# Attention products with one input in PSUM, GpSimd products in short pieces, replanned dummies and one opening load queue

## The chip, the cores and the metric

One NeuronCore of a Trainium2 chip runs the whole kernel. Its engines are TensorE (PE; its weight loads are PEld), VectorE (DVE), ScalarE (ACT), GpSimd (POOL) and SyncE (SP). The metric is device time in microseconds (us) of one execution. A profile is taken from one more execution; its span leaves out a little time at either end.

## What is computed

Two blocks in a row: linear attention with a quadratic sketch as its feature map, and then a feed-forward layer with the activation h - tanh(h). Batch 4, 4 heads, sequence 1088, head size 32, sketch size 8; 4352 tokens of width 128, hidden width 2048; all float32 at the ends.

```python
def phi(x):                                   # S1, S2: 8 x 32
    a = np.einsum('rd,bhsd->bhsr', S1, x)
    b = np.einsum('rd,bhsd->bhsr', S2, x)
    return np.einsum('bhsi,bhsj->bhsij', a, b).reshape(*x.shape[:-1], 64)
q_p, k_p = phi(q), phi(k)
kv, z = np.einsum('bhsf,bhsd->bhfd', k_p, v), np.sum(k_p, axis=2)
num = np.einsum('bhsf,bhfd->bhsd', q_p, kv)
den = np.einsum('bhsf,bhf->bhs', q_p, z)[..., None] + 1e-06
x = num / den                                 # laid out as 4352 x 128
h = x @ w_in                                  # 128 x 2048
out = (h - np.tanh(h)) @ w_out                # 2048 x 128
```

## The kernel before

**A planner writes the order.** Every operation is entered with P.op: engine, estimated cost in ns, the data it reads and writes (from which its dependencies follow), and a priority (`prio`, lower is sooner, in slots of the feed-forward layer). `listed` lays the operations out on the five engines by these costs, starting at each step the ready operation with the lowest priority; VectorE may stay idle for a short while (HOLD) if a more urgent operation is about to be ready. `schedule` repeats this six times and keeps the shortest plan. `P.line` adds an order by hand between tagged operations. `sync` puts in the semaphore waits; each engine then runs its list strictly in order. So what the plan puts ahead of an instruction is ahead of it on the chip, however long it takes there. A load is modelled as 2000 ns after its issue plus its size on one shared bus.

**Work by group.** The 34 chunks of 32 tokens of each batch are split into three groups (SIZES: 8, 14, 12 in batch 0, and so on), twelve in all, g = 0 to 11. A group of n = 256 to 448 columns has: p{g} (16 small PE matmuls, `quarters`, L589) that project q into PSUM banks 0 and 1; VectorE's transposition qq (L618), product au (L621), sum dn (L624); a PE matmul ds (L631) into bank 2; VectorE's reciprocal rd (L634) and scaling an (L636, both inputs in SBUF); the outer products qp (L641), one half on GpSimd and one on VectorE, in one instruction each; their transpositions qpT (L648); w{g} (16 matmuls, L602) into banks 2 and 3; and the cast xT (L655, tags x{g}). w{g} and p{g+1} are one operation of the plan, so the cast of x{g} waits for both.

**Keys by batch** (`keys`, `sums_of`). kT (L484) transposes the keys, 8 + 8 or 16 PE matmuls project them (L491) into banks 0 and 1, kab (L502) transposes that into SBUF. From kab come the 64 products per token and head, wk (L509): both inputs are views of kab in SBUF. In batch 0 VectorE makes parts 0 to 1, 2 to 3 and 4 of nine, GpSimd 5 to 8 in one instruction; later VectorE makes three parts and GpSimd six, in one instruction each. Beside it gram (L520), mask product gm (L527, one input in PSUM), fold (L534) and u (L539) fill in a part of wq that p needs. sums (L551, 72 matmuls, needs all of wk and v), kvz, turn and ndw (L557 to L563) give the matrix that w needs.

**Feed-forward** (`layers`). Per group sixteen matmuls L710 (w_in) into one of three PSUM banks, sixteen tanh on ScalarE (L713), and sixteen matmuls L721 (w_out) that accumulate in bank 7 with a lag of 12 slots; the linear part h @ w_out is a precomputed product (wt, wc, wp at L675 to L686; whi and wlo) added with two matmuls L702. Then osb (L728) and four stores.

**Opening.** The S matrices are loaded on SP, k of batch 0 on ScalarE's queue, q of the first group and w_in on SP, v split over both. 90 dummy matmuls on zeros (L445, priority 5000, planned at 107 ns) fill PE where the plan has nothing else. The sketch matrix pS (L449) and wkm (L452) stand ahead of all key work; for VectorE a line gives wkm, kT00, kT01, qT0, s2m, kab0, wk00, gm0, wk02, u0, wk04, qq0 and on; for PE pS to w1p2.

## Time and profile before

| | us |
|---|---|
| median of three runs | 125.65 (124.51 to 125.68) |
| the profiled execution | 126.7 |
| its span | 124.2 |
| TensorE, VectorE, ScalarE, GpSimd busy in it | 110.0, 77.1, 80.5, 32.6 |
| start of the first xT cast | 20.95 |

All times in rows are us from the start of the span unless marked ns. "idle before <-releaser" is how long the engine did nothing ahead of a row, and what ended that; "issue" there means that the profile shows nothing it waited for. A row that groups instructions gives the first start and the time over which they lie. PE ends are modelled, so a busy PE is not PE at its peak. PEclk is the granted TensorE clock as a share of its full 2.4 GHz; 0.50 is the other level, 1.2 GHz.

### The profile page before, as it was taken

The numbers are of one execution on the slowest core, as the hardware profiler recorded it, in microseconds if no ns is written. First come the engines' busy times: TensorE is split into PE (matmuls) and PEld (weight loads), VectorE is DVE, ScalarE is ACT, GpSimd is POOL, SyncE is SP. The second block draws the span as 40 slices with busy tenths as digits, with TensorE's granted clock in tenths as the row PEclk, the third lists the DMA queues.
The fourth block names the chain that finished last, engine by engine and source line by source line (L and its number), as shares of the span: only waits on it lengthen the run. The fifth ranks groups of instructions, "written<-read, shape, count | busy, mean of one in ns | idle before, by whom it ended". The sixth has DMA issues, their size and how long they took to land.

```text
span 124.2 us, 3347 instructions
## 1 busy us (share of the span) xinstructions
PE 110.0 (89%) x1392; PEld 62.8 (51%) x1392; DVE 77.1 (62%) x170; ACT 80.5 (65%) x207; POOL 32.6 (26%) x40
## 2 busy tenths in 40 slices
...
DMA packets 24623, 11.23 MB, mean 90 GB/s; under 512 B 18720, under 2 KB 22944, under 8 KB 24608
## 3 DMA queue, kind: packets, MB, share of 16 engines
...
q10 hardware_dynamic: 576, 0.82, 2.2%
...
q14 instruction: 4, 0.03, 0.1%
...
## 4 chain that ended last, share of the span: by engine, by line
PE 66%; DVE 19%; ACT 6%; issue 3%; POOL 2%; DVEq 0%
PE ps L710 18%; PE ps L721 18%; PE ps L445 8%; DVE wk L509 6%; ACT tt L713 6%; PE ps L602 5%; DVE an L636 4%; PE ps L551 4%; PE ps L589 3%; PE ps L702 3%; PE ps L491 3%; DVE kab L502 3%; POOL qp L641 2%; DVE qpT L648 1%; DVE osb L728 1%
## 5 line engine op out<-in xcount | busy, mean ns | idle before, releaser
L713 ACT ACTIVATE tt<-ps 128x384 bf16<-128x384 f32 (+3 forms) x192 | 73.6, 500 | 19.0 <-PE ps L710 18.7
L710 PE MATMUL ps<-xT,w_in 128*128 128x384 bf16 (+3 forms) x192 | 58.8, 322 | 1.1 <-ACT tt L713 0.3
L721 PE MATMUL ps<-tt,w_out 128*128 128x384 bf16 (+3 forms) x192 | 53.2, 322 | 0.0
L710 PEld LDWEIGHTS ps<-xT,w_in 128*128 128x128 bf16 x192 | 18.3, 98 | 24.6 <-ACT tt L713 15.4
L641 POOL TENSOR_TENSOR qp<-an,qq 128x384 f32<-128x384 f32 (+3 forms) x12 | 13.9, 1159 | 57.9 <-DVE an L636 57.9
L721 PEld LDWEIGHTS ps<-tt,w_out 128*128 128x128 bf16 x192 | 19.4, 102 | 8.7 <-issue 2.5
L509 POOL TENSOR_TENSOR wk<-kab 128x1536 f32<-128x1536 f32 (+1 forms) x4 | 12.4, 3110 | 13.6 <-DVE kab L502 13.6
L445 PE MATMUL ps<-wz 128*128 128x256 bf16 x90 | 13.7, 301 | 2.1 <-DVE hmask L422 1.1
L648 DVE STREAM_TRANSPOSE qpT<-qp 128x384 f32<-128x384 f32 (+3 forms) x24 | 13.0, 545 | 1.0 <-POOL qp L641 0.2
L655 DVE CAST xT<-ps 128x384 bf16<-128x384 f32 (+3 forms) x12 | 6.4, 536 | 11.6 <-PE ps L589 11.6
L445 PEld LDWEIGHTS ps<-wz 128*128 128x128 bf16 x90 | 9.1, 108 | 5.5 <-issue 2.5
L728 DVE STREAM_TRANSPOSE osb<-ps 128x384 f32<-128x384 f32 (+3 forms) x12 | 6.4, 535 | 7.2 <-PE ps L710 4.5
L634 DVE RECIPROCAL rd<-ps 128x24 f32<-128x24 f32 (+3 forms) x12 | 3.6, 297 | 11.2 <-PE ps L631 11.1
L509 DVE TENSOR_TENSOR wk<-kab 128x768 f32<-128x768 f32 (+2 forms) x6 | 8.6, 1436 | 0.1
L636 DVE TENSOR_TENSOR an<-qq,rd 128x96 f32<-128x96 f32 (+3 forms) x12 | 7.4, 619 | 0.4
L589 PE MATMUL ps<-qT,wq 64*32 64x192 f32 (+3 forms) x192 | 6.6, 331 | 1.1 <-DVE wq L539 1.1
L618 DVE STREAM_TRANSPOSE qq<-ps 128x384 f32<-128x384 f32 (+3 forms) x12 | 6.6, 549 | 0.3 <-PE ps L589 0.3
L602 PE MATMUL ps<-qpT,ndw 64*32 64x192 f32 (+3 forms) x192 | 6.6, 328 | 0.2
L641 DVE TENSOR_TENSOR qp<-an,qq 128x384 f32<-128x384 f32 (+3 forms) x12 | 6.4, 535 | 0.4
L557 ACT COPY kvz<-ps 128x128 f32<-128x128 f32 x4 | 1.1, 266 | 8.2 <-PE ps L551 8.2
L573 DVE STREAM_TRANSPOSE qT<-qraw 128x384 f32<-128x384 f32 (+3 forms) x12 | 6.2, 518 | 0.0
L702 PE MATMUL ps<-xT,whi 128*128 128x384 bf16 (+3 forms) x12 | 3.9, 321 | 2.5 <-DVE osb L728 2.5
...
## 6 DMA issues: line engine op xcount, KB each, us to landing
...
w_in_f<-in_moe_w_in_dram SPq DMA_DIRECT2D x4, 256.0 KB, 5.4
...
```

The lines of the kernel that those rows point to most:

```text
L445: P.op("tensor", cost, lambda e: e.matmul(ps[:, 6, 0:256], wz[:, 0:128], wz[:, :], start=True, stop=True), r=[("wz",)], w=[bank[6]], prio= ...
L509: P.op(eng, (dve if eng == "vector" else pool)(64 * n), lambda e: e.tensor_tensor(out=wk[:, t0:t1, :, :].rearrange("p t h (i j) -> p (t h) ...
L589: ins = e.matmul(ps[32 * s:32 * s + 32, r, 0:32 * nh], wq[64 * r:64 * r + 64, b, y, :, :].rearrange("p h x -> p (h x)"), qT[i][64 * r:64 * ...
L602: ins = e.matmul(ps[32 * h:32 * h + 32, 2 + u, 0:32 * nh], ndw[i][64 * u:64 * u + 64, 32 * h:32 * h + 32], src[64 * u:64 * u + 64, h // 2, ...
L636: P.op("vector", dve(4 * n), lambda e: e.tensor_tensor(out=an[u][:, 0:n, :], in0=a[:, 0:n, 0:4], in1=rd[u][:, 0:n, None].to_broadcast([128 ...
L641: P.op("gpsimd" if r else "vector", (pool if r else dve)(32 * m), lambda e, lo=lo, m=m: e.tensor_tensor(out=qp[u][:, lo:lo + m, :].rearran ...
L648: P.op("vector", dve(32 * m), lambda e, lo=lo, m=m: e.transpose(out=qpT[u][:, 32 * lo:32 * (lo + m)], in_=qp[u][:, lo:lo + m, :].rearrange ...
L702: P.op("tensor", pe(n), lambda e, x=x, f=front and x is whi, l=not front and x is wlo: e.matmul(acc[:, 0:n], x[:, :], xT[:, t0:t0 + n], st ...
L710: P.op("tensor", pe(n), lambda e, jb=jb, bk=bk: e.matmul(bk[:, 0:n], w_in[:, 128 * jb:128 * jb + 128], xT[:, t0:t0 + n], start=True, stop= ...
L713: P.op("scalar", act(n), lambda e, ts=ts, bk=bk: e.activation(out=tt[:, ts, 0:n], in_=bk[:, 0:n], func=AF.Tanh, scale=-1.0), r=[kb], w=[(" ...
L721: P.op("tensor", pe(n), lambda e, jb=jb, ts=ts: e.matmul(acc[:, 0:n], w_out[:, jb, :], tt[:, ts, 0:n], start=(jb == 0 and not g), stop=(jb ...
L728: P.op("vector", dve(n), lambda e: e.transpose(out=osb[u][:, 0:n], in_=acc[:, 0:n]), r=[ka], w=[("osb", u)], prio=slot0)
```

## The change

- **Products with an input in PSUM.** In batch 0 VectorE transposes the first 256 columns of the projection a second time, into PSUM bank 2 (kps), and its two remaining wk products take their second input there. rd is now written to PSUM, so `an` reads one input there. For groups 0 and 1 `an` is cut in two, and the half that VectorE multiplies on itself lies in PSUM too.
- **GpSimd.** In batch 0 it makes wk part 4, parts 5 to 6 and parts 7 to 8, in three instructions; in later batches all nine parts in nine. From group 2 on it makes both halves of qp.
- **Banks and order.** ds moves to bank 0; the keys of later batches use banks 2 and 3; qq has two buffers in place of three. w{g} and p{g+1} are two operations, in this order. wt0 stands ahead of sums0 and wt1 ahead of turn0 on PE, wc0 ahead of kvz0 and wc1 ahead of ndw0 on ScalarE.
- **Dummies.** 80 in place of 90, planned at 213 ns for the first 17 and 125 after. One is not started if an urgent operation will be ready within its cost, and all that the plan has after w0 are dropped (`trim`).
- **Loads.** Loads of one queue keep the order in which they are entered. q of the first group and all of v for batch 0 move to ScalarE's queue behind k; the first w_in load waits until k has landed. The planner's load model is 1400 ns after issue, with rates by kind of load.

```diff
+    def trim(self):
+        order = self.schedule()["tensor"]
+        n = order.index(self.tags["w0"])
+        late = {o for o in order[n:] if o.prio >= FILL}
...
-            if o.sem is None and e in HELD:
+            if o.sem is None and (e in HELD or o.prio >= FILL):
                 hold = None
+                most = 1.0 if o.prio >= FILL else HOLD
...
-        o = P.op(eng, size / 330, fn, w=() if also else keys, sem=sem, prio=prio)
+        chain = queue.setdefault(eng, [])
+        o = P.op(eng, size / rate, fn, r=r, w=() if also else keys, sem=sem, prio=prio)
...
+        if chain:
+            o.order.add(chain[-1])
...
-        return ((0, 2), (2, 4), (4, 5), (5, 9)) if b == 0 else ((0, 3), (3, 9))
+        return ((0, 2), (2, 4), (4, 5), (5, 7), (7, 9)) if b == 0 else tuple((t, t + 1) for t in range(9))
...
-            (-24, -990), (-15, -985), (-14, -980), (-12, -960), (-12, -975), (-11, -970))]
-        kb = bank[0:2]
-        gb = 4 if b == 0 else 1
+            (-24, -990), (-15, -985), (-14, -980), (-2, -960), (-12, -975), (-11, -970))]
+        k0 = 2 if b else 0
+        kb = bank[k0:k0 + 2]
+        gb = 4 if b == 0 else 3
...
+        if b == 0:
+            P.op("vector", dve(256), lambda e: e.transpose(
+                out=ps[:, 2, 0:256].rearrange("p (t r x) -> p r t x", t=4, r=2),
+                in_=ps[:, 0:2, 0:128].rearrange("p r (t j) -> p r t j", j=32)),
+                r=kb, w=[bank[2]], prio=T[2], tag="kps")
...
-            ab = kab[:, t0:t1, :, :, :, :].rearrange("p t r h i x -> p (t r h) i x")
+            ab = bv = kab[:, t0:t1, :, :, :, :].rearrange("p t r h i x -> p (t r h) i x")
+            if eng == "vector":
+                bv = ps[:, 2, 64 * t0:64 * t1].rearrange("p (n i x) -> p n i x", i=R, x=2)
...
-            mul("gpsimd" if t1 == 9 else "vector", t0, t1, T[3])
+            mul("vector" if b == 0 and t1 <= 4 else "gpsimd", t0, t1, T[3])
...
+        half = g < 2
+        p_rd, p_an = ps[:, 0, 288:288 + n], ps[:, 1, 256:256 + 4 * m].rearrange("p (n x) -> p n x", x=4)
...
+                out=out, in0=a[:, lo:hi, 0:4], in1=p_rd[:, lo:hi, None].to_broadcast([128, hi - lo, 4]), op=ALU.mult),
...
-            P.op("gpsimd" if r else "vector", (pool if r else dve)(32 * m), lambda e, lo=lo, m=m: e.tensor_tensor(
+            dv = half and not r
+            P.op("vector" if dv else "gpsimd", (dve if dv else pool)(32 * m), lambda e, lo=lo, dv=dv: e.tensor_tensor(
...
-    warm(90, 107, 5000)
+    warm(80, 5000)
     load_k(0, -2995, "scalar")
-    load_q(0, -2990, (0,))
-    load_v(0, -2980, ("sync", "scalar", "sync", "scalar"))
+    load_q(0, -2990, (0,), "scalar")
+    load_v(0, -2980, ("scalar",) * 4)
     for x in range(4):
-        load_w_in(x, -960)
+        load_w_in(x, -960, [("kraw", 0, 1)] if x == 0 else ())
...
-        quarters([("w", g)] + ([("p", g + 1)] if g + 1 < NG else []), T)
+        quarters([("w", g)], T)
         x_of(g, T)
+        if g + 1 < NG:
+            quarters([("p", g + 1)], T + 0.1)
+            P.line([f"w{g}", f"p{g + 1}"])
...
-    P.line(["cin0", "cin1", "cin2", "cin3", "kvz0", "ndw0", "wc0", "wc1"])
-    P.line(["wk05", "qp01", "cout0", "cout1"])
+    P.line(["cin0", "cin1", "cin2", "cin3", "wc0", "kvz0", "wc1", "ndw0"])
+    P.line(["wk04", "wk05", "wk07", "qp01", "cout0", "cout1"])
```

## Rows read from the trace of the kernel before

**Rows 1.** The page, busy us, share of the span and instructions of each engine
```profile
PE 110.0 (89%) x1392; PEld 62.8 (51%) x1392; DVE 77.1 (62%) x170; ACT 80.5 (65%) x207; POOL 32.6 (26%) x40
```

**Rows 2.** Chain of waits that ended last, shares by line, from the page
```profile
PE ps L710 18%; PE ps L721 18%; PE ps L445 8%; DVE wk L509 6%; ACT tt L713 6%; PE ps L602 5%; DVE an L636 4%; PE ps L551 4%; PE ps L589 3%; PE ps L702 3%; PE ps L491 3%; DVE kab L502 3%; POOL qp L641 2%; DVE qpT L648 1%; DVE osb L728 1%
```

**Rows 3.** Windows: stretch, length, busy us (count) by engine, clock, DMA share, GB/s
```profile
20.95:28.46 7.51, 7.15 (x97) 4.79 (x95) 5.94 (x14) 5.58 (x17) 1.40 (x1) 1.00 0.68 167
28.46:39.99 11.53, 9.25 (x104) 4.11 (x103) 10.02 (x17) 7.35 (x16) 4.04 (x2) 0.96 0.25 63
39.99:48.41 8.42, 8.25 (x132) 4.02 (x131) 4.53 (x11) 5.59 (x15) 1.22 (x1) 0.86 0.40 88
48.41:54.96 6.55, 6.50 (x67) 3.20 (x66) 4.61 (x12) 6.24 (x16) 1.22 (x1) 1.00 0.33 97
54.96:65.81 10.85, 9.41 (x112) 4.90 (x111) 8.85 (x16) 6.94 (x17) 4.63 (x2) 1.00 0.17 26
```

**Rows 4.** Timeline of the opening: start us, us, engine, line, what [idle before <-releaser]
```profile
1.05 6.14 PE L445 MATMUL ps<-wz 128*128 128x256 bf16 x38 [1.05 <-DVE hmask L422]
7.44 0.19 DVE L452 TENSOR_TENSOR wkm<-ps,hmask 128x32 f32<-128x32 f32 x1 [4.88 <-PE ps L449]
7.55 1.36 DVE L484 STREAM_TRANSPOSE kT<-kraw 128x576 f32<-128x576 f32 x2
9.75 0.69 PE L491 MATMUL ps<-kT,wkm 64*32 64x288 f32 x8
10.51 0.78 DVE L502 STREAM_TRANSPOSE kab<-ps 128x576 f32<-128x576 f32 x1 [1.09 <-PE ps L491]
11.32 0.69 DVE L509 TENSOR_TENSOR wk<-kab 128x512 f32<-128x512 f32 x1
11.38 2.44 POOL L509 TENSOR_TENSOR wk<-kab 128x1024 f32<-128x1024 f32 x1 [1.61 <-DVE kab L502]
11.99 0.19 DVE L527 TENSOR_TENSOR gm<-ps,bmask 128x32 f32<-128x32 f32 x1
12.10 2.27 DVE L509 TENSOR_TENSOR wk<-kab 128x512 f32<-128x512 f32 x1
14.50 0.45 PE L589 MATMUL ps<-qT,wq 64*32 64x128 f32 x16 [1.09 <-DVE wq L539]
18.92 1.16 PE L445 MATMUL ps<-wz 128*128 128x256 bf16 x9 [1.05 <-issue]
20.00 0.45 PE L602 MATMUL ps<-qpT,ndw 64*32 64x128 f32 x16
```

**Rows 5.** Opening's loads: issue and cast (timeline), size and us to landing (DMA)
```profile
0.73 0.86 ACTq L386 DMA_DIRECT2D kraw<-in_k_dram  x2
8.05 2.62 ACT L661 CAST w_in<-w_in_f 128x512 bf16<-128x512 f32 x4 [4.18 <-DMA w_in_f<-in_moe_w_in_dram]
...
kraw<-in_k_dram ACTq DMA_DIRECT2D x1, 256.0 KB, 3.1
out_dram<-osb SPq DMA_DIRECT2D x8, 32.0 KB, 1.7
```

**Rows 6.** Timeline of the first stage that makes keys
```profile
33.70 2.82 POOL L509 TENSOR_TENSOR wk<-kab 128x1536 f32<-128x1536 f32 x1 [0.25 <-DVE kab L502]
34.00 3.33 DVE L509 TENSOR_TENSOR wk<-kab 128x768 f32<-128x768 f32 x1
37.49 0.62 PE L534 MATMUL ps<-gm,s2m 128*128 128x16 f32 x4 [2.03 <-DVE gm L527]
```

**Rows 7.** Windows: one us out of the stretch at half clock, columns as above
```profile
40.00:41.00 1.00, 1.00 (x4) 0.38 (x3) 1.00 (x3) 0.00 (x0) 0.00 (x0) 0.50 0.00 0
```

**Rows 8.** Tile view (ns min/median/max) of an; groups by form of two lines
```profile
L636 DVE TENSOR_TENSOR an<-qq,rd x12: 224/258/2449, 17.0 to 108.8; 128x96 f32<-128x96 f32 x6, 128x64 f32<-128x64 f32 x2, 128x112 f32<-128x112 f32 x2, 128x80 f32<-128x80 f32 x2
...
L641 POOL TENSOR_TENSOR qp<-an,qq 128x384 f32<-128x384 f32 x6 | 7.3, 1218 | 37.1 <-DVE an L636 37.1
L713 ACT ACTIVATE tt<-ps 128x256 bf16<-128x256 f32 x32 | 9.3, 405 | 0.9 <-PE ps L710 0.9
```

102 lines of the change are left out of this document (56 added, 46 removed).

## The prediction

> **What bounds the kernel now.** Begin with the busy times [rows 1]: TensorE is busy 110.0 of 124.2 us, ScalarE 80.5, VectorE 77.1, GpSimd 32.6. The chain that ended last [rows 2] says the same by line: L710, L721 and the dummies of L445 lead, but L509 and L636, two products on VectorE, hold 11% of it although they are short work. The table by stage [rows 3], whose edges are the starts of consecutive xT casts, shows where. A plain stage of 384 columns (48.41 to 54.96) takes 6.55 us with PE busy 6.50: nothing to win there. The stage from 54.96 makes keys for a later batch and takes 10.85 with PE busy 9.41; a second of its kind (from 79.58) repeats it. The first stage with keys (28.46) takes 11.53 with 9.25. So three stages have some 5 us of open idle time, and the opening takes 20.95 us before the first xT.
>
> The opening [rows 4], in order: 38 dummies run to 7.19, and the tiny sketch matmul stands behind them on PE, so wkm starts at 7.44 and the key transposes at 7.55. The k load had landed long before: its two pieces are issued from 0.73, the second by about 1.2, and need 3.1 us [rows 5], so 4.3. kab starts at 10.51. Then GpSimd's product runs 11.38 to 13.82; VectorE's second product starts at 12.10 and takes 2.27 where the first, of equal size, took 0.69, and ends 0.55 after GpSimd's. The mask product gm at 11.99, with one input in PSUM, ran its 0.19 in the middle of that same GpSimd instruction. The pair stands again in the first keys stage [rows 6]: GpSimd 33.70 to 36.52, VectorE's product from 34.00 takes 3.33 and ends 0.81 after it; gm waits behind it on VectorE, the fold matmul waits for gm, PE is idle 2.03 us, and soon after the clock is at its half level [rows 7]. And `an`, 0.26 by its median, takes 2.45 at worst [rows 8], once in each later keys stage. I read this as: a VectorE product of two SBUF tensors waits for a running GpSimd product; one with a PSUM input does not.
>
> **The change, part by part.**
> *Dummies.* The 38 were planned at 107 ns (4.07 us) and took 6.14. At 213 each, about ten fit before the sketch matrix S is due. Its landing has no row; a 32 KB transfer takes 1.7 us and 256 KB of k 3.1 [rows 5], so from an issue near 1.2 it lies between 2.9 and 4.3. I take 3.6, since it shares the transfer engines with k. Then the sketch matmul, wkm at 3.9, key transposes 4.1 to 5.5 (1.36, as now), the last projection 0.15 and 0.69 later [rows 4]: kab at 6.3, and 7.0 if PE still runs at half rate there. I take 6.8: 3.7 earlier. Ends: 6.2 and 7.8.
>
> *From kab to p0.* Now 3.99 us (10.51 to 14.50). After: kab 0.81; a second transpose, into PSUM, 0.42 (the key transposes move 1088 columns in 1.36, so 256 cost 0.32 by size, more with their start); product 0.70; gm 0.20; product 0.70 with the fold matmul (0.62 [rows 6]) beside it; u and the step to p0 0.4, two short instructions like gm: 3.3 in all. Gain 0.7. What VectorE gives up goes to GpSimd in three pieces: 1536 elements took 2.82 [rows 6], so 256 cost 0.47 by size, and 0.81 by the 1.22 of 384 [rows 8], which contain a wait. I take 0.56, and 1.0 for 512. All are done 2.75 after kab, at p0 + 0.3; sums0 stands behind p0 and the transposes of w_in on PE, which hide that.
>
> *From p0 to w0.* Now 5.50 us, and directly ahead of w0 stand nine dummies (1.16) and, before them, 1.05 in which PE waited for nothing shown. I take away the 1.05 and 0.3 of the dummies, since VectorE's transposes end only shortly before. Added: eight w_in transposes now ahead of sums0 (nine dummies of twice their columns took 1.16, so 0.55) and `an` cut in two (its smallest form is 0.22, so +0.2). 4.9; gain 0.6. Ends: 1.3, and -0.3 if the unexplained microsecond comes back.
>
> *w and p apart.* xT waits only for w: w's 0.45 and a step of 0.1 instead of 0.95. Gain 0.4 once; in later groups PE's lagged products cover the cast, so nothing.
>
> *One load queue.* k, the first q and v go through ScalarE's queue (seven issues of 0.43, as the two of k), and w_in waits on SP until k has landed, at 4.3. As many bytes precede the last w_in piece as now, so I put its landing where it is: casts from 8.05 [rows 5], four in 2.62. They are needed after p0, near 10.1. Costed at nothing, covered by that slack; if w_in is 2 us later, the transposes and sums0 behind them are 1 to 2 later. SP's chain behind w_in (q, w_out, the next k, v, q) has its first user after dn0.
>
> Opening: 3.7 + 0.7 + 0.6 + 0.4 = 5.4 earlier at x0.
>
> *The stages.* Stage 0 takes 7.51; ScalarE's sixteen tanh need 16 x 0.405 = 6.5 [rows 8], so 6.9: 0.6. Stage 1 has 2.28 idle; VectorE makes no wk there any more, so gm and fold come when kab does: 2.0. Stage 2's mean clock of 0.86 means 2.4 of its 8.42 us at half rate, 1.2 lost; the idle before it goes: 1.0. In each of the two later keys stages `an` loses 2.2 of waiting. The gain there is at least the idle (1.44) and at most down to a plain stage plus the keys' matmuls (6.55 + 0.69 [rows 4] + 0.62 [rows 6] = 7.86), 3.0; I take 2.1 each, 4.2. Sum 7.8.
>
> *What is late next.* GpSimd. A keys batch becomes nine pieces of 0.56 with gaps of 0.06, 5.6 us instead of 2.8, and from group 2 on both halves of qp are its own. The 384-element row is 1.22, but it starts beside VectorE's half; by the rate of 1536 it is 0.80. Two take 1.66, so each group's chain to w grows by 0.45, and xT returns about 0.35. That chain (two transposes and x near 0.57, six short steps near 0.3, 1.66, w) is 5.7 by estimate and fits into the 6.50 of PE's plain stage: hidden. In the keys stages a product waits behind a piece, once or twice 0.56: I give back 0.5 in each of three, 1.5. Keys now use banks 2 and 3, so w waits for u; u comes some 3 us after the projection, w later: nothing. The tail after the last xT is not touched.
>
> Sum: 124.2 - 5.4 - 7.8 + 1.5 = 112.5 of span. The profiled execution took 126.7, 2.5 around its span, so 115.0; the median of the three runs, 125.65, lies 1.05 below it: **114.0**.
>
> **Rivals.**
> *GpSimd becomes the late engine.* If its order puts the nine pieces ahead of qp, a keys stage is kab at about 3.3, pieces 5.6, halves 1.7, transposing and w 1: over 11 us, no shorter than now. The gains of stages 1, 4 and 7 (6.2) go, with the 1.5 counted in: 118.7. For: 1.84 ns per element (2.82 for 1536) against VectorE's 1.35 (0.69 for 512). Against: products can slip between short pieces, and sums are needed only a stage later. The Trainium skill (GPSIMD Engine Reference, 4.1 Engine selection) advises VectorE for elementwise work because GpSimd is about half as fast with two inputs. The rates here differ by 1.4; by that advice the time is this rival's 118.7.
>
> *The opening is bound by its loads.* The profile cannot show how fast one queue alone brings k and v. If half the opening's gain goes, 2.7: 116.7.
>
> *The PSUM input doesn't spare the wait.* gm's 0.19 speaks against it, but that is 32 elements. Then the opening's two products wait for pieces (0.5 and 1.0) and `an` in three stages about 0.6: 117.3. The pieces are short, so most of the gain stays even so.
>
> *The clock; slower than before.* With no dummies after w0, PE stands idle between tanh in stages 0 and 1. In the trace the rate fell to half after 2.03 us of idleness [rows 6, 7]. Each microsecond of PE work at half rate costs another; to eat 11.7 and 1% more, it must hold for 13 us, from w0 nearly to the end of stage 1, and then the time is 127 or more. Against: PE is busy 7.15 of 7.51 in stage 0 [rows 3], and the one spell did not renew itself. The Trainium skill (TensorE: Matmul & The Clock Gate, HAM oscillation) says that repeated gaps can bring the slow state back each time; in this trace it came once.
>
> **How the numbers follow.** My sum 0.62 (its own range 111 to 117), GpSimd 0.13, loads 0.12, no spared wait 0.05, clock 0.03, 0.05 for what I do not see. The low end, 110.5, takes the better ends: 1.5 more in the opening, 1.8 in the keys stages, and part of the 1.5 not given back. The high end, 119.5, takes in all rivals but the clock. One per cent is about what can be told from no change: faster 0.92, same 0.04, slower 0.04.
>
> **What would show it.** wkm before 4.5 and kab before 7.5; VectorE's products at 0.7 in the opening beside running GpSimd pieces; no `an` over 0.5; w0 near 15, x0 near 15.5; keys stages near 8.7 with no idle before the fold; no half rate after the opening. Wrong would be: GpSimd busy through the keys stages with w waiting for qpT, idle PE before sums0 on a load, or a stage at half clock.

## The result, and the profile after

The changed kernel takes 120.31 us (median of 4 runs, 119.9 to 121.27), the kernel before 125.39 beside it: the ratio is 0.9617, with a 95% interval of 0.9537 to 0.9698. It is faster by 3.8%, 5.1 us; the forecast was 114.0, its range 110.5 to 119.5. The direction held; the size did not, and the time lies above the range. Ratios, here and below, compare only executions within 1.5% of their kernel's fastest; medians are over all. The profiled execution took 119.9, its span is 118.1.

The account first, in three parts with the same marks as in the sum of the prediction (start of the first xT cast, of the fourth, end of the span):

| stretch | before | forecast | after | after less forecast |
|---|---|---|---|---|
| opening, to x0 | 20.95 | 15.55 | 16.30 | +0.75 |
| x0 to x3 (stages 0 to 2, with 0.5 of the 1.5 given back) | 27.46 | 24.36 | 26.29 | +1.93 |
| x3 to the end of the span | 75.79 | 72.59 | 75.51 | +2.92 |
| span | 124.2 | 112.5 | 118.1 | +5.6 |

So nearly all of the gain is in the opening (4.65 us). The stretch from x3 on, where the forecast took 3.2 net, gave 0.3, and that only behind the last output transposition: up to it the stages are 0.63 longer than before (71.97 against 71.34 us, in the table of the experiments), and what is left of the span is 0.91 shorter, which no run here explains. The page of after, busy time of each engine [rows 1], and its chain of waits that ended last [rows 2]:

```profile
PE 105.3 (89%) x1347; PEld 58.2 (49%) x1347; DVE 62.8 (53%) x159; ACT 80.7 (68%) x207; POOL 43.8 (37%) x76
...
DMA kraw<-in_k_dram 17%; PE ps L744 13%; PE ps L755 12%; ACT tt L747 11%; POOL wk L533 10%; DMA qraw<-in_q_dram 6%; PE ps L575 3%; PE ps L626 3%; PE ps L736 3%; POOL qp L675 3%; DVE kT L500 2%; DVE qT L597 1%; SPq L423 1%; DVE xT L689 1%; DVE kab L518 1%
```

VectorE's products and `an`, L509 and L636 in the old chain, are no longer among its larger lines. In their place stand loads (k 17%, q 6%) and GpSimd's pieces of wk (10%). The opening of after, timeline of VectorE and of TensorE (start us, us, engine, line, what, idle before and what ended it), to be held against [rows 4]:

```profile
6.90 0.78 DVE L518 STREAM_TRANSPOSE kab<-ps 128x576 f32<-128x576 f32 x1 [0.80 <-PE ps L507]
8.07 0.69 DVE L533 TENSOR_TENSOR wk<-kab,ps 128x512 f32<-128x512 f32 x1
8.86 0.68 DVE L533 TENSOR_TENSOR wk<-kab,ps 128x512 f32<-128x512 f32 x1
13.20 0.65 DVE L597 STREAM_TRANSPOSE qT<-qraw 128x448 f32<-128x448 f32 x1 [1.47 <-DMA qraw<-in_q_dram]
...
6.73 1.67 PE L460 MATMUL ps<-wz 128*128 128x256 bf16 x7
8.63 0.83 PE L460 MATMUL ps<-wz 128*128 128x256 bf16 x6
11.42 0.62 PE L709 MATMUL ps<-identb,w_in 128*128 128x128 bf16 x8 [0.78 <-ACT w_in L695]
15.75 0.45 PE L626 MATMUL ps<-qpT,ndw 64*32 64x128 f32 x16
15.99 0.56 PE L613 MATMUL ps<-qT,wq 64*32 64x224 f32 x5
18.27 0.60 PE L613 MATMUL ps<-qT,wq 64*32 64x224 f32 x11 [1.72 <-issue]
18.80 0.50 PE L744 MATMUL ps<-xT,w_in 128*128 128x256 bf16 x3
```

Both products take 0.7 although GpSimd's pieces run beside them from 7.78 to 10.69. But TensorE waits 0.78 for the casts of w_in (its first piece landed at 9.06 and its last at 12.05, before at 8.03 and 10.03), ahead of the transposes that now stand before sums0. VectorE waits 1.47 for the second part of q. And TensorE stops for 1.72 in the middle of p1, waiting for nothing the profile shows: the first matmul of L744 starts 2.64 earlier than before, not 4.65. Further on, two transposes of late keys on VectorE wait for their load:

```profile
27.11 0.71 DVE L500 STREAM_TRANSPOSE kT<-kraw 128x512 f32<-128x512 f32 x1 [1.01 <-DMA kraw<-in_k_dram]
...
35.19 0.71 DVE L500 STREAM_TRANSPOSE kT<-kraw 128x512 f32<-128x512 f32 x1 [2.37 <-DMA kraw<-in_k_dram]
35.82 0.52 DVE L689 CAST xT<-ps 128x384 bf16<-128x384 f32 x1
```

The cast x2 stands behind the second. Last the windows (columns as in [rows 3]): the second keys stage and the stage behind it, of before and then of after.

```profile
54.96:65.81 10.85, 9.41 (x112) 4.90 (x111) 8.85 (x16) 6.94 (x17) 4.63 (x2) 1.00 0.17 26
65.81:73.20 7.39, 7.24 (x139) 4.45 (x138) 4.60 (x12) 5.67 (x17) 1.22 (x1) 1.00 0.12 19
```

```profile
50.55:58.30 7.75, 7.70 (x114) 4.20 (x102) 5.66 (x15) 6.01 (x15) 3.79 (x6) 1.00 0.14 22
58.30:67.98 9.68, 8.99 (x162) 5.09 (x146) 4.17 (x11) 7.01 (x21) 5.01 (x8) 1.00 0.18 28
```

The keys stage is 3.10 shorter, the stage behind it 2.29 longer, and has 23 more matmuls: 18.24 for the two became 17.43. The next pair went from 18.64 to 18.36.

### The profile page after: what moved, and what is told of

The parts are those of the page before. It is cut to its first block, busy times and chain, and to the rows that moved or that the text cites. A ratio compares the mean times of both kernels' runs of the same rounds, so it can differ in the third digit from the quotient of the medians.

```text
span 118.1 us, 3285 instructions
## 1 busy us (share of the span) xinstructions
PE 105.3 (89%) x1347; PEld 58.2 (49%) x1347; DVE 62.8 (53%) x159; ACT 80.7 (68%) x207; POOL 43.8 (37%) x76
## 3 DMA queue, kind: packets, MB, share of 16 engines
q10 hardware_dynamic: 1008, 1.25, 3.7%
## 4 chain that ended last, share of the span: by engine, by line
PE 36%; DMA 23%; POOL 12%; ACT 11%; DVE 10%; issue 2%; SPq 1%; ACTq 0%; POOLq 0%; DVEq 0%
DMA kraw<-in_k_dram 17%; PE ps L744 13%; PE ps L755 12%; ACT tt L747 11%; POOL wk L533 10%; DMA qraw<-in_q_dram 6%; PE ps L575 3%; PE ps L626 3%; PE ps L736 3%; POOL qp L675 3%; DVE kT L500 2%; DVE qT L597 1%; SPq L423 1%; DVE xT L689 1%; DVE kab L518 1%
## 5 line engine op out<-in xcount | busy, mean ns | idle before, releaser
L744 PE MATMUL ps<-xT,w_in 128*128 128x384 bf16 (+3 forms) x192 | 59.0, 320 | 2.6 <-DVE xT L689 1.6
L675 POOL TENSOR_TENSOR qp<-an,qq 128x384 f32<-128x384 f32 (+3 forms) x22 | 17.9, 812 | 43.7 <-DVE an L663 42.6
L744 PEld LDWEIGHTS ps<-xT,w_in 128*128 128x128 bf16 x192 | 18.5, 99 | 27.1 <-ACT tt L747 16.2
L533 POOL TENSOR_TENSOR wk<-kab 128x256 f32<-128x256 f32 (+1 forms) x30 | 19.8, 658 | 14.2 <-DVE kab L518 12.0
L659 DVE RECIPROCAL ps<-ps 128x24 f32<-128x24 f32 (+3 forms) x12 | 3.7, 305 | 11.1 <-PE ps L656 10.9
L460 PE MATMUL ps<-wz 128*128 128x256 bf16 x45 | 8.4, 342 | 1.1 <-DVE hmask L437 1.1
L500 DVE STREAM_TRANSPOSE kT<-kraw 128x576 f32<-128x576 f32 (+1 forms) x8 | 5.7, 721 | 3.4 <-DMA kraw<-in_k_dram 3.4
L460 PEld LDWEIGHTS ps<-wz 128*128 128x128 bf16 x45 | 4.8, 118 | 3.4 <-issue 1.1
L575 PE MATMUL ps<-wk,vx 128*32 128x64 f32 x288 | 4.8, 220 | 1.3 <-POOL wk L533 1.3
L695 ACT CAST w_in<-w_in_f 128x512 bf16<-128x512 f32 x4 | 2.5, 618 | 4.9 <-DMA w_in_f<-in_moe_w_in_dram 4.8
L575 PEld LDWEIGHTS ps<-wk,vx 128*32 128x32 f32 x288 | 4.2, 110 | 2.3 <-POOL wk L533 2.0
L613 PEld LDWEIGHTS ps<-qT,wq 64*32 64x32 f32 x192 | 3.6, 107 | 2.6 <-issue 2.1
```

Source lines behind the costliest of these rows:

```text
L460: P.op("tensor", 213 if x < 17 else 125, lambda e: e.matmul(ps[:, 6, 0:256], wz[:, 0:128], wz[:, :], start=True, stop=True), r=[("wz",)], ...
L500: P.op("vector", dve(32 * (hi - lo)), lambda e, lo=lo, hi=hi: e.transpose(out=kT[i][:, 32 * lo:32 * hi], in_=kraw[i][:, 32 * lo:32 * hi]), ...
L533: P.op(eng, (dve if eng == "vector" else pool)(64 * n), lambda e: e.tensor_tensor(out=wk[:, t0:t1, :, :].rearrange("p t h (i j) -> p (t h) ...
L575: ins = e.matmul(ps[32 * h:32 * h + 32, sbk, 0:64], vx[i][:, h, t, :], wk[:, t, h, :], start=(t == 0), stop=(t == 8), tile_position=(0, 32 ...
L613: ins = e.matmul(ps[32 * s:32 * s + 32, r, 0:32 * nh], wq[64 * r:64 * r + 64, b, y, :, :].rearrange("p h x -> p (h x)"), qT[i][64 * r:64 * ...
L675: P.op("vector" if dv else "gpsimd", (dve if dv else pool)(32 * m), lambda e, lo=lo, dv=dv: e.tensor_tensor(out=qp[u][:, lo:lo + m, :].rea ...
```

## The experiments

Sixteen kernels, each timed against the kernel before on the same chip. "x0 to x3" and "x3 to end" (the end of the last output transpose) are from each profile, us; a stop of TensorE that falls ahead of x0, as in e1_pad, is not in them.

| kernel | what | median us | ratio to before | x0 to x3 | x3 to end |
|---|---|---|---|---|---|
| before | | 125.4 to 125.9 | 1 | 27.46 | 71.34 |
| after | | 120.31 | 0.9617 [0.9537, 0.9698] | 26.29 | 71.97 |
| e2_late | late keys' transposes behind x2, x3 | 116.75 | 0.9398 [0.9338, 0.9457] | 23.74 | 72.11 |
| e3_loads | opening loads in two queues | 120.15 | 0.9671 [0.9584, 0.9757] | 24.25 | 71.95 |
| e12_dummies | dummies planned as before | 118.76 | 0.9476 [0.9338, 0.9614] | 23.91 | 71.70 |
| e1_pad | 26 tiny matmuls more | 120.12 | 0.9546 [0.9423, 0.9669] | 23.30 | 71.89 |
| e8_wide | half as many, wider dummies | 121.52 | 0.9777 [0.9685, 0.9869] | 25.24 | 72.01 |
| e5_half | VectorE makes half of qp | 117.39 | 0.9416 [0.9348, 0.9484] | 25.47 | 70.00 |
| e13_half_sbuf | the same from SBUF | 118.57 | 0.9542 [0.9477, 0.9607] | 23.72 | 71.47 |
| e7_sbuf | no PSUM inputs | 119.52 | 0.9617 [0.9529, 0.9705] | 26.57 | 71.96 |
| e9_long | no short pieces | 118.41 | 0.9517 [0.945, 0.9584] | 27.71 | 69.63 |
| e15_long_sbuf | neither | 120.05 | 0.9597 [0.9533, 0.9662] | 27.85 | 71.28 |
| e14_undo | e7, e12 and e3 together | 119.23 | 0.9538 [0.9438, 0.9637] | 23.40 | 71.69 |
| b1_gps | before + wk on GpSimd | 128.01 | 1.0296 [1.0226, 1.0366] | 23.56 | 77.15 |
| b2_psum | the same + `an` from PSUM | 122.01 | 0.9803 [0.9742, 0.9864] | 23.66 | 71.15 |
| e6_both | e2 and e5 | 115.13 | 0.9224 [0.9142, 0.9307] | 21.59 | 70.44 |
| e10_three | e2, e5 and e8 | 114.95 | 0.9233 [0.9122, 0.9344] | 21.55 | 70.34 |
| e11_four | e2, e5, e8 and e3 | 114.41 | 0.9232 [0.9138, 0.9325] | 21.16 | 70.34 |

### Late loads behind an earlier opening: e2_late, e3_loads, e12_dummies

**e2_late.**
```diff
+    P.line(["x2", "kT21"])
+    P.line(["x3", "kT31"])
```


> The changed kernel with two order constraints: the transposes of the third and fourth batch's keys on VectorE (kT21, kT31) come behind the casts x2 and x3 instead of ahead of them. In the changed kernel they wait there for the k load (1.01 us at 27.11, 2.37 us at 35.19), and au2 with osb0, and x2, stand behind them. Theory A (these waits are part of what ate the gain): both waits leave VectorE, x2 comes 1.5 to 2.3 earlier than 35.82, ScalarE's idle of 1.98 before the tanh of stage 2 goes, and 1.5 to 2.5 us of it stay to the end: 117.8 to 118.8. Rival B (the stages behind are held by something else, such as GpSimd's chain, which takes the gain back): x2 earlier, but the time within 0.5 of 120.3.

Measured: 0.9398, against 0.9617 for the changed kernel. Both waits are gone; x2 has nothing of a load ahead of it, and the first keys stage has TensorE busy throughout (timeline of VectorE; windows of the stage, 8.12 busy of 8.19):

```profile
32.03 0.56 DVE L689 CAST xT<-ps 128x384 bf16<-128x384 f32 x1 [0.96 <-PE ps L626]
...
23.84:32.03 8.19, 8.12 (x118) 4.20 (x102) 5.59 (x14) 7.25 (x16) 4.03 (x6) 1.00 0.76 169
```

x0 to x3 is 2.55 shorter, x3 to the end 0.14 longer. Theory A holds, at its upper end or a little past it: the two waits, 3.38 us in all, cost about 2.4 by the profiles and 2.7 by the ratios.

**e3_loads.**
```diff
-    load_q(0, -2990, (0,), "scalar")
-    load_v(0, -2980, ("scalar",) * 4)
+    load_q(0, -2990, (0,))
+    load_v(0, -2980, ("sync", "scalar", "sync", "scalar"))
-        load_w_in(x, -960, [("kraw", 0, 1)] if x == 0 else ())
+        load_w_in(x, -960)
```


> The changed kernel with the opening loads in two queues again, as before the change: q's first part on SP, v's four pieces by turns on SP and ScalarE, and w_in no longer waiting for k. All else, the order on PE, VectorE and GpSimd too, is that of the changed kernel. Theory A (one queue and the wait for k cost later loads about 2 us: the last w_in piece landed at 12.05 instead of 10.03, k of the second batch 20.01 instead of 16.89, k of the third 27.09 instead of 24.85): w_in lands 1 to 2 us earlier, the later k loads 2 us earlier, the waits of kT21 and kT31 shrink from 1.01 and 2.37 to under 0.5 each, and the time falls by 0.5 to 2.0 us: 118.3 to 119.8. Rival B (that the wait kept k early, and that the opening pays for it): k's second half lands later than 4.0, kab starts over 0.5 later than 6.90, and the time is 120.3 or more, up to 121.5.

Measured: 0.9671, no different from the changed kernel. In its profile the loads do come earlier (the last w_in piece lands at 10.61 instead of 12.05, k of the fourth batch at 33.18 instead of 35.16), one of the two waits of kT is gone, and x0 to x3 is 2.04 shorter. The timed runs, 118.61 to 122.35, don't show that gain, and the profiled one is the fastest of them. Whether one queue costs anything by itself stays open; it isn't more than the intervals, about 1 us either way.

**e12_dummies.**
```diff
-            P.op("tensor", 213 if x < 17 else 125, lambda e: e.matmul(
+            P.op("tensor", 107, lambda e: e.matmul(
-    warm(80, 5000)
+    warm(110, 5000)
```


> The changed kernel with its dummies planned at 107 ns each again, as before the change: 65 in place of 45 up to p1, ten of the added ones ahead of the sketch matmul, four more ahead of wkm; nothing else changes up to the first L744. The opening then starts later: wkm near 7 instead of 4.0, kab near 9.5 instead of 6.9, first L744 2 to 3 us later than 18.80. Theory A (the opening's gain is partly eaten in the changed kernel by the loads of later batches, which come no earlier: kT21 and kT31 waited 1.01 and 2.37 us for them): the waits of kT shrink by as much as the opening is later, x2 comes less than 1 us later than 35.82, and the time is 0 to 1 us longer, 120.3 to 121.3. Rival B (the opening's gain is whole): 2 to 3 us longer, 122.3 to 123.3.

Measured: 0.9476; neither expectation came true, though the interval overlaps the changed kernel's. The sketch matmul starts 1.9 later than in the changed kernel (5.46 instead of 3.55) and kab 1.24 later (8.14), as meant, and yet the first L744 comes earlier, at 17.55 instead of 18.80:

```profile
16.77 0.58 PE L613 MATMUL ps<-qT,wq 64*32 64x224 f32 x15
17.55 0.50 PE L744 MATMUL ps<-xT,w_in 128*128 128x256 bf16 x3 [0.20 <-DVE xT L689]
```

The second part of q has landed when VectorE comes to it (12.70, no wait), and TensorE's stop shrinks from 1.72 to 0.37. So the last 1.2 us by which the new plan brings kab forward are worth nothing in this kernel: what follows waits for loads and for the stop. Executions with one and the same order up to x0 say so too: in e5_half and e2_late p0 starts at 9.27 and 10.62, and w0 at 15.12 and 15.04. In the first of them TensorE waits 0.87 for w_in and VectorE 1.76 for q, in the second nothing and 0.25. Most of the opening's gain doesn't hang on the price of a dummy: at 107 each, 21 stand ahead of the sketch matmul here and 38 did in the kernel before, since the change also gave the planner new times for the loads and a new rule for starting a dummy.

### TensorE's stop: e1_pad, e8_wide

Both kernels stop after exactly their 221st matmul: before, among the dummies at 17.87 (the unexplained 1.05 of [rows 4]); after, in p1 at 16.55. In the trace, a packet of 16 KB of kind "instruction" starts 2.76 us before TensorE goes on in the changed kernel, and 3.00 in the kernel before.

**e1_pad.**
```diff
+    P.op("tensor", 100, lambda e: [e.matmul(
+        ps[0:32, 3, 0:16], wz[:, 0:32], wz[:, 0:16], start=True, stop=True) for _ in range(26)][-1],
+        r=[("wz",)], w=[bank[3]], prio=-964.5, tag="pad")
+    P.line(["p0", "pad"])
```


> The changed kernel with one addition: 26 tiny matmuls (16 columns each) on TensorE between p0 and wt0, where it stood idle from 10.65 to 11.42 us anyway. Nothing else moves. In both kernels TensorE stops for 1 to 1.7 us, waiting for nothing the profile shows, after exactly 221 matmuls: before, that point lay among the dummies ahead of w0 (17.87 to 18.92); after, it lies inside p1 (16.55 to 18.27). Theory A (it is the fetch of TensorE's own instructions, so the place is set by the count of instructions): the stop moves 26 matmuls earlier, into the dummies at 14.2 to 15.7; p1 runs through, the first matmul of L744 starts near 17.2 instead of 18.80, and the time falls by 1.0 to 1.7 us, to 118.6 to 119.3. Rival B (the stop belongs to p1's own inputs or to a moment, not to a count): it stays at 16.5 to 18.3, 18.80 stays, time 120.3 within 0.5. Rival C (the stop moves but the time is set later, by the key stages): first L744 near 17.2, time 120.3 within 0.5.

Measured: 0.9546, not to be told from the changed kernel. The stop did move by the count, to after the 221st matmul, which is now a dummy ahead of w0:

```profile
14.14 1.04 PE L460 MATMUL ps<-wz 128*128 128x256 bf16 x8
17.52 0.71 PE L460 MATMUL ps<-wz 128*128 128x256 bf16 x5 [2.34 <-issue]
18.16 0.45 PE L626 MATMUL ps<-qpT,ndw 64*32 64x128 f32 x16
...
19.20 0.77 PE L744 MATMUL ps<-xT,w_in 128*128 128x256 bf16 x3 [0.21 <-DVE xT L689]
```

That is against B: a count sets the place. But the packet starts at 14.91, only 0.6 earlier than in the changed kernel (15.51), and TensorE, there earlier, just waits longer. The first L744, at 19.20, isn't earlier than 18.80; the expectation of 17.2 was wrong. After the stop the clock is at its lower level as well (granted 0.51 from 19.20 to 22.70, where the changed kernel has 1.00).

**e8_wide.**
```diff
-            P.op("tensor", 213 if x < 17 else 125, lambda e: e.matmul(
-                ps[:, 6, 0:256], wz[:, 0:128], wz[:, :], start=True, stop=True), ...
+            P.op("tensor", 426 if x < 8 else 235, lambda e: e.matmul(
+                ps[:, 6, :], wz[:, 0:128], wz[:, None, :].to_broadcast([128, 2, 256]), start=True, stop=True), ...
-    warm(80, 5000)
+    warm(40, 5000)
```


> The changed kernel with its dummies twice as wide (512 columns) and half as many: 25 instead of 45 up to p1. Nothing else changes up to the first L744. Theory A (TensorE stops after its 221st matmul, some 2.5 to 3 us after the 16 KB fetch of instructions starts, whose place among the matmuls stays about 20 ahead): with 20 fewer matmuls the 221st lies among the L744 of stage 0, of 0.13 to 0.4 us each, where 20 of them last longer than the fetch; p1 runs through, the first L744 comes near 17.2 instead of 18.80, and the time falls by 1.0 to 1.7 us: 118.6 to 119.3. Rival B (the fetch starts by the clock or by another engine's place, not by TensorE's count): a stop of 1 to 2 us stays in p1 or just behind it, time within 0.5 of 120.3. Rival C (the stop just goes to the first L744 and costs the same there): first L744 near 17.2, first tanh of stage 0 held later instead, 120.3.

Measured: 0.9777, slower than the changed kernel, with intervals that just touch. The stop is gone, and the first L744 is where A put it. But the planner set kT21 ahead of x1 here, and it waits for the load:

```profile
16.18 0.61 PE L613 MATMUL ps<-qT,wq 64*32 64x224 f32 x16
17.00 0.50 PE L744 MATMUL ps<-xT,w_in 128*128 128x256 bf16 x3 [0.20 <-DVE xT L689]
...
25.07 0.71 DVE L500 STREAM_TRANSPOSE kT<-kraw 128x512 f32<-128x512 f32 x1 [2.93 <-DMA kraw<-in_k_dram]
25.71 0.59 DVE L689 CAST xT<-ps 128x448 bf16<-128x448 f32 x1
```

1.8 us are won at the first L744, and by x1, one stage later, the kernel is 1.2 behind (25.71 instead of 24.53). TensorE is idle for 2.52 ahead of its first matmul of that stage, and the clock falls to its lower level in it (granted 0.57 from 26.36 to 30.00). Even so this profiled execution took 119.09, less than the changed kernel's 119.9; the other five took 120.87 to 122.78, at granted clocks of 0.963 to 0.977 where this one has 0.978. No trace of those five was kept, so what made them longer isn't shown; more of the lower clock is the one sign on record. With 19 fewer matmuls ahead of stage 0 the 222nd starts 2.56 after the packet without a pause; this and e1_pad together show that the number of matmuls sets the place of the stop. What sets the start of the packet isn't shown: over the eighteen kernels between 144 and 221 matmuls had started by then. That it is the fetch of TensorE's instructions is argued from the packets' times; no run takes the fetch away with the count left alone.

### GpSimd's share: e5_half, e13_half_sbuf

**e5_half.**
```diff
-        half = g < 2
+        half = True
```


> The changed kernel with VectorE making one half of qp from PSUM in every group, as the changed kernel does only in the first two; GpSimd makes the other half. Theory A (two qp halves of 0.9 us each on GpSimd, with nine pieces of 0.64 among them, make the chain to w late in the stages with keys and behind them; VectorE waits there for POOL qp 8.4 us in all): the waits of qpT for POOL shrink by half, the stages from x4 to x6 (17.43) and x7 to x9 (18.36) come down by 0.5 to 1 each, and the time falls by 1 to 2 us: 118.3 to 119.3. Rival B (VectorE has no room: 0.63 us more of it per group makes it late for tanh's follow-up and the casts): 120.3 to 122. Rival C (TensorE and ScalarE bind and the chain is hidden): within 0.5 of 120.3.

Measured: 0.9416, theory A. x3 to the end is 1.97 shorter. VectorE's waits in that stretch, of after and then of this kernel (us in total, times, longest):

```profile
DVE qpT L682 <- POOL qp L675: 7.1, 9, 1.3
```

```profile
DVE qpT L682 <- POOL qp L675: 0.8, 2, 0.4
```

The pairs of a keys stage and the one behind it take 16.81 and 17.16, where after has 17.43 and 18.36. In the first pair the gain is in the stage behind the keys stage (8.85 in place of 9.68), in the second in the keys stage itself (7.63 in place of 8.76); qp and the pieces of wk meet on GpSimd in both.

**e13_half_sbuf.** e5_half with the edit of e7_sbuf below.

> The changed kernel with VectorE's half of qp in every group (alone: ratio 0.9416 where the changed kernel has 0.9617), but with every VectorE product reading SBUF alone: reciprocal, an and keys' products as in the run with the PSUM inputs taken away (alone: 0.9617, where the two opening products took 0.88 and 1.40 in place of 0.69 and 0.68, and VectorE's halves 0.85 and 1.36 in place of 0.42 and 0.62). Theory A (the PSUM input is what lets VectorE make a half of qp beside GpSimd's): VectorE's half takes 1.0 to 1.4 in place of 0.56 in each group, up to 0.6 more on the chain to w, and at least half of the gain of 0.020 goes: ratio 0.950 to 0.965. Rival B (what helped is the shorter work on GpSimd, and the longer product is hidden under TensorE's plain stages): ratio 0.938 to 0.948.

Measured: 0.9542, theory A. VectorE's half takes 1.18 by its median where it took 0.56 (tile view, ns min/median/max, e5_half and then this kernel), and 1.47 of the 1.97 from x3 to the end are gone:

```profile
L675 DVE TENSOR_TENSOR qp<-ps,qq x12: 423/557/624, 13.7 to 100.1; 128x384 f32<-128x384 f32 x6, 128x256 f32<-128x256 f32 x2, 128x448 f32<-128x448 f32 x2, 128x320 f32<-128x320 f32 x2
```

```profile
L676 DVE TENSOR_TENSOR qp<-an,qq x12: 846/1184/1357, 15.5 to 102.5; 128x384 f32<-128x384 f32 x6, 128x256 f32<-128x256 f32 x2, 128x448 f32<-128x448 f32 x2, 128x320 f32<-128x320 f32 x2
```

It is the PSUM input that makes VectorE's half beside GpSimd's pay. The changed kernel had the means and used them in two groups of twelve.

### PSUM inputs and short pieces: e7, e9, e15, b1, b2, e14

**e7_sbuf.**
```diff
-                bv = ps[:, 2, 64 * t0:64 * t1].rearrange("p (n i x) -> p n i x", i=R, x=2)
+                bv = ab
-        p_rd, p_an = ps[:, 0, 288:288 + n], ps[:, 1, 256:256 + 4 * m].rearrange("p (n x) -> p n x", x=4)
+        p_rd, p_an = rd[u][:, 0:n], an[u][:, 0:m, :]
```


> The changed kernel with the PSUM inputs of VectorE's products taken away: the opening's two products read both inputs from kab in SBUF (the transpose into PSUM still runs, its result unread), the reciprocal is written to SBUF, and an and VectorE's half of qp in the first two groups read SBUF alone. Theory A (a product of two SBUF tensors waits for a running GpSimd product, one with a PSUM input doesn't): the second opening product takes up to 1.3 us in place of 0.68 and ends with a GpSimd piece, an takes up to 0.9 beside a piece (0.24 now) and qp's half likewise; the pieces being 0.64 long, each costs 0.3 to 0.6, on the path in the opening and in the key stages: 0.5 to 1.5 us longer, 120.8 to 122. Rival B (it is not the input's place but the length of GpSimd's instruction or another thing that made the long products of before): products stay at 0.7 and 0.24, time within 0.5 of 120.3.

Measured: 0.9617, the same as the changed kernel. The mechanism shows all the same, in the opening's two products (0.69 and 0.68 with the PSUM input):

```profile
8.03 0.88 DVE L534 TENSOR_TENSOR wk<-kab 128x512 f32<-128x512 f32 x1
...
8.98 1.40 DVE L534 TENSOR_TENSOR wk<-kab 128x512 f32<-128x512 f32 x1
```

GpSimd's three pieces stretch too, to 3.56 from 2.91. But what is lost is at most 0.5 us at wq in the opening (10.37 instead of 9.85; in e2_late, with PSUM inputs, it starts at 10.28), ahead of the load and the stop that wait there anyway, and `an` takes 0.32 at worst: it meets no long piece. A on the mechanism, B on the time.

**e9_long.**
```diff
-        return ((0, 2), (2, 4), (4, 5), (5, 7), (7, 9)) if b == 0 else tuple((t, t + 1) for t in range(9))
+        return ((0, 2), (2, 4), (4, 5), (5, 7), (7, 9)) if b == 0 else ((0, 3), (3, 9))
```


> The changed kernel with GpSimd's nine short pieces of the later batches put together into two (three parts and six of nine, 768 and 1536 elements); the first batch as it is. Theory A (short pieces let qp slip between them): a qp half waits for up to 2.8 us more behind the long piece, xT of that stage comes 1 to 2.5 later in three stages, 1.5 to 4 us longer, 122 to 124. Rival B (with no lock the length doesn't matter, since the planner puts the long pieces where no qp is due; the gaps of 0.06 between pieces are saved): within 0.7 of 120.3.

Measured: 0.9517; by the timed runs no slower, so theory A is wrong. x3 to the end is 2.34 shorter and x0 to x3 1.42 longer, with a spell of half clock in it, right behind TensorE's stop, of 1.87 here (the mean granted clock of x0 to x3 is 0.94). That spell ends at 22.5, before the first piece that the edit changed (31.52), so it isn't the pieces' doing.

**e15_long_sbuf.** e9_long with the edit of e7_sbuf.

> The changed kernel with two parts undone together, each of which alone cost nothing: GpSimd's nine short pieces of the later batches put together into two (768 and 1536 elements; alone 0.9517), and VectorE's products reading SBUF alone (alone 0.9617). Theory A (short pieces and PSUM inputs are two covers for one wait, and either suffices: with short pieces a product that waits for a running GpSimd instruction waits 0.6 at most, with a PSUM input it doesn't wait at all): with both gone an takes 1 to 2.8 us in the later key stages, as in the kernel before (2.45 at worst), and the time is 1.5 to 4 us over the changed kernel, ratio 0.975 to 0.995. Rival B (in the changed kernel's order an never stands beside a wk product): an stays under 0.35 and the ratio at 0.95 to 0.965.

Measured: 0.9597. A's mechanism shows and its time doesn't. In the profiled execution, with 120.91 the longest of its six, `an` waits again, in both later keys stages (1.17 and 1.48, where e9_long has 0.24), and the table's 1.65 from x3 to the end against e9_long are those stages:

```profile
55.54 1.17 DVE L664 TENSOR_TENSOR an<-qq,rd 128x80 f32<-128x80 f32 x1
...
79.69 1.48 DVE L664 TENSOR_TENSOR an<-qq,rd 128x80 f32<-128x80 f32 x1
```

So each of the two parts spares `an` the wait, and with one there the other does nothing for it: for `an`, that is why neither cost anything when it was undone alone. Against the changed kernel the pair together comes out at nothing too; that the loss is paid by the 2.3 us that long pieces gained from x3 on in e9_long is the reading, not a test.

**b1_gps**, on the kernel before:
```diff
-            mul("gpsimd" if t1 == 9 else "vector", t0, t1, T[3])
+            mul("gpsimd" if b or t1 == 9 else "vector", t0, t1, T[3])
```


> The kernel before with one edit: GpSimd also makes the first third of the later batches' wk (768 elements), which VectorE made there; VectorE has no wk product left in the key stages. No short pieces, no PSUM input, the old opening. Theory A (VectorE's product of 3.33 us in stage 1, behind which gm and the fold stood, was the loss): stage 1 comes from 11.5 to 9.5 and its 2.03 us of idle TensorE goes, with the half clock behind it 1 us more: 2 to 3 us, 122.5 to 123.5. Against it an, from SBUF, meets a longer GpSimd stretch and may take 2.5 to 4 in the key stages, giving 1 to 2 back. Rival B (the division alone brings nothing, since an pays for it): within 0.7 of 125.5.

**b2_psum**, the same and:
```diff
-        P.op("vector", 60 + 8.3 * n, lambda e: e.reciprocal(rd[u][:, 0:n], ps[:, 2, 256:256 + n]),
+        P.op("vector", 60 + 8.3 * n, lambda e: e.reciprocal(ps[:, 2, 288:288 + n], ps[:, 2, 256:256 + n]),
-            out=an[u][:, 0:n, :], in0=a[:, 0:n, 0:4], in1=rd[u][:, 0:n, None].to_broadcast([128, n, 4]), op=ALU.mult),
+            out=an[u][:, 0:n, :], in0=a[:, 0:n, 0:4], in1=ps[:, 2, 288:288 + n, None].to_broadcast([128, n, 4]), op=ALU.mult),
```


> The kernel before with that edit and a second: the reciprocal stays in PSUM, and an reads it there. Theory A (a PSUM input spares an the wait): an takes 0.26 everywhere, each later key stage (10.85 and 10.91 before) loses its 1.44 and 1.28 us of idle TensorE: 1.5 to 3 us under the one edit alone. Rival B (that idle isn't an's doing, or comes back a stage later): within 0.7 of the one edit.

Measured: 1.0296 and 0.9803. The division of work alone makes the kernel slower, outside both expectations: the first keys stage falls from 11.53 to 8.48, more than was expected, but the later ones take 12.77 and 15.75 (10.85 and 10.91 before). Reading the reciprocal from PSUM gives 6.0 us back by the medians, far more than the 1.5 to 3 expected: 11.00 and 11.61. Not all of that is the wait alone: in b1_gps TensorE is idle for 3.75 in the last keys stage, waiting for gm on VectorE, and the clock is at its lower level behind it (granted 0.50 from 86.7 to 90.0); b2_psum has no such spell. Tile views of `an` and of VectorE's qp, b1_gps and then b2_psum:

```profile
L636 DVE TENSOR_TENSOR an<-qq,rd x12: 224/258/1477, 16.9 to 108.8; 128x96 f32<-128x96 f32 x6, 128x64 f32<-128x64 f32 x2, 128x112 f32<-128x112 f32 x2, 128x80 f32<-128x80 f32 x2
L641 DVE TENSOR_TENSOR qp<-an,qq x12: 425/558/3112, 17.2 to 109.0; 128x384 f32<-128x384 f32 x6, 128x256 f32<-128x256 f32 x2, 128x448 f32<-128x448 f32 x2, 128x320 f32<-128x320 f32 x2
```

```profile
L636 DVE TENSOR_TENSOR an<-qq,ps x12: 220/254/256, 17.9 to 104.5; 128x96 f32<-128x96 f32 x6, 128x64 f32<-128x64 f32 x2, 128x112 f32<-128x112 f32 x2, 128x80 f32<-128x80 f32 x2
L641 DVE TENSOR_TENSOR qp<-an,qq x12: 424/558/1440, 18.2 to 104.7; 128x384 f32<-128x384 f32 x6, 128x256 f32<-128x256 f32 x2, 128x448 f32<-128x448 f32 x2, 128x320 f32<-128x320 f32 x2
```

The one line on `an` takes its worst case from 1.48 to 0.26; qp, still from SBUF, keeps a wait (1.44 at worst, where it had 3.11). In the kernel before, whose long pieces stand in the way, the PSUM input is worth more than any other single edit measured here.

**e14_undo**, the edits of e7_sbuf, e12_dummies and e3_loads together.

> The changed kernel with three of its parts undone together: dummies planned at 107 ns, the opening loads in two queues with w_in not waiting for k, and VectorE's products reading SBUF alone. Each undone by itself left the time where it was or lower (ratios 0.9476, 0.9671, 0.9617; the changed kernel 0.9617). What stays is GpSimd making all of the later batches' wk in short pieces and both halves of qp, the order with the w_in transposes ahead of sums0, and w apart from p. Theory A (the three parts share one bound in the opening, loads and the stop after matmul 221, so that one alone shows nothing): together they cost 1.5 to 3.5 us, ratio 0.972 to 0.99. Rival B (the gain over the kernel before comes from the rest, the new division of work between VectorE and GpSimd): ratio 0.945 to 0.968.

Measured: 0.9538, rival B: three parts undone together cost nothing either. Its x0 is at 17.35, still 3.6 ahead of the kernel before. What gives that gain isn't one of the three; of it, the 38 dummies ahead of the sketch matmul that became 21 with the planner's new load times and its new rule for starting one are the part that the timeline shows (5.64 instead of 7.13). How the rest divides among the first batch's new shares, the trimmed dummies and the moved w_in transposes was not tried.

### Together: e6_both, e10_three, e11_four

> The changed kernel with both edits that helped alone: kT21 and kT31 behind x2 and x3, and VectorE making one half of qp from PSUM in every group. Alone they gave ratios to the kernel before of 0.9398 and 0.9416 where the changed kernel had 0.9617. Theory A (two separate losses, the waits of kT up to x2 and GpSimd's chain behind x3): the gains add to 4 to 5 us, ratio 0.915 to 0.925, 115 to 116 us at a kernel before of 125.6; from x3 to the end TensorE is idle under 1 us, as with the halves alone (0.7 to 1.5 by the table of two stretches), and x0 to x3 takes under 24 us. Rival B (one loss told twice, the stages behind x3 being held by TensorE's own work either way): ratio 0.935 to 0.945, 117 to 118.5 us.

> The changed kernel with three edits: kT21 and kT31 behind x2 and x3, VectorE's half of qp from PSUM in every group, and the dummies twice as wide and half as many. The first two together gave a ratio of 0.9224. Wide dummies alone took away TensorE's stop after its 221st matmul (first L744 at 17.00 in place of 18.80) but lost the time again at once, because kT21 then stood ahead of x1 on VectorE and waited 2.93 us for the third batch's k. Theory A (the stop's 1 to 1.8 us is a loss of its own, and stays saved where no transpose of late keys stands in front): first L744 near 17.0, x0 to x3 under 22.5 us, the time 0.7 to 1.7 us under the two edits alone: ratio 0.909 to 0.917. Rival B (something later in the first stages, loads or TensorE's own work, takes it back): ratio 0.918 to 0.928.

> The kernel with three edits (late kT21 and kT31, VectorE's half of qp everywhere, wide dummies) and, as a fourth, the opening loads in two queues as before the change, w_in not waiting for k. Alone, the two queues brought w_in and the later loads 1 to 2 us earlier, and the time no lower (ratio 0.9671). Theory A (what the later loads were needed for was the early kT, which now is late): within 0.5 us of the three edits. Rival B (w_in's landing, behind which TensorE stood 0.8 to 1.35 us idle before its transposes, and the first q's 1.47 us, bind the opening once the rest is gone): 0.6 to 1.5 us under the three edits. Rival C (k comes later when v and q share the start): kab 0.3 to 0.6 later than 6.9, and 0.3 to 1 us longer.

Measured: 0.9224, 0.9233 and 0.9232. The edits of e2_late and e5_half add, as A of e6_both has it: 115.13 us. Wide dummies on top take the stop away (first L744 at 16.91 in e10_three), but the timed runs show no more than 0.2 us of it, and two queues no more than another 0.5: for e10_three and e11_four the intervals can't tell A from B. In e6_both's profile the stop isn't there either. There p0 came early (9.32), TensorE waited 1.35 for w_in, the clock was at its lower level from 11.3 to 14.5 (granted 0.50), so that sums0 took 2.15 instead of 1.21, and TensorE reached its 221st matmul after the packet had landed; the delays at this place stand in for one another. All three beat both kernels. Windows of before, after, e5_half and e10_three, x0 to x3 and x3 to the end:

```profile
20.95:48.41 27.46, 24.65 (x330) 12.91 (x328) 20.48 (x42) 18.53 (x48) 6.65 (x4) 0.94 0.42 99
48.41:119.75 71.34, 67.62 (x802) 37.52 (x800) 46.24 (x100) 56.78 (x151) 16.39 (x10) 1.00 0.20 35
```

```profile
16.30:42.59 26.29, 21.52 (x326) 11.67 (x321) 16.69 (x40) 17.50 (x47) 11.13 (x15) 1.00 0.59 145
42.59:114.56 71.97, 69.50 (x821) 37.37 (x805) 37.12 (x90) 57.23 (x152) 24.16 (x34) 1.00 0.23 42
```

```profile
41.15:111.15 70.00, 68.52 (x822) 37.20 (x806) 41.70 (x106) 57.80 (x153) 17.68 (x26) 1.00 0.24 43
```

```profile
16.43:37.98 21.55, 20.51 (x309) 11.09 (x293) 16.95 (x44) 16.79 (x45) 9.32 (x13) 1.00 0.71 171
37.98:108.32 70.34, 68.86 (x823) 37.41 (x822) 42.24 (x108) 58.27 (x154) 17.69 (x26) 1.00 0.24 43
```

TensorE's idle time is length less its busy time. From x3 to the end it is 3.72 us before, 2.47 after, 1.48 in both others. Little else was to win in the second stretch. In the first it is 2.81 before, 4.77 after and 1.04 in e10_three.

## Why the prediction was wrong, point by point

**To p0, right.** kab came at 6.90 (6.8 was taken), p0 at 10.19 (10.1), and VectorE's products took 0.7. The sum had "7.0 if PE still runs at half rate there", and it did: the trace records the clock only from 8.26 on, but seven dummies from 6.73 take 0.24 each and six from 8.63 take 0.14. In e5_half, with the same order and a record from 4.72 on, kab comes at 6.27. w to xT is 0.55 in place of 0.95, as costed.

**p0 to w0, failed.** The step took away "the 1.05 and 0.3 of the dummies" and came to 4.9; it took 5.56. VectorE's second q transpose waited 1.47 for its load, which landed at 13.17 (11.15 before). TensorE waited 0.78 for w_in ahead of sums0, one of the prediction's own signs of being wrong. "One load queue", "costed at nothing, covered by that slack", is the step that failed: "I put its landing where it is" gave w_in's last piece 10.03, and it landed at 12.05; what stands behind w_in on SP, q, was not asked about at all. In this profile either wait alone would have held the reciprocal (13.77) to within 0.3 of where it is, by estimate: ds0, behind sums0, ends at 13.51, and the q transposition at 13.85. Without them the step was sized well: e3_loads takes 4.42 from p0 to w0 and e12_dummies 4.61. How much of the waiting the queue makes, and how much is just that the consumers came earlier, e3_loads leaves open, since its p0 came 1.25 later; e12_dummies shows that with kab 1.24 later both waits are gone at no cost. A single profile is no exact measure here: in six kernels with the same order up to x0 (the changed one, e2_late, e3_loads, e5_half, e6_both, e9_long) w0 starts at 15.04 to 16.77.

**The unexplained microsecond, failed, and mis-sized.** It was to vanish, with "-0.3 if the unexplained microsecond comes back". It came back as 1.72, and not between p0 and w0 but in p1, where the 221st matmul now is: 45 dummies lie ahead of it where 74 did (e1_pad and e8_wide show that the count sets the place). It stood among dummies before, where nothing but dummies waited; now it lies between x0 and its first matmul.

**Stages 0 to 2, mis-sized by a wait that was not in the sum.** They were to take 24.36 and took 26.29: 8.23, 11.29 and 6.77 where the sum had 6.9, 9.5 and 7.4 with 0.5 given back. In the 26.29 the stop is 1.72 and the two kT waits about 2.4 (e2_late); without those waits stage 1's own gain is larger than the 2.0 taken (8.19 in e2_late against 11.53 [rows 3]). The prediction had named SP's chain behind w_in and said that it "has its first user after dn0", but not that the users, planned earlier, would overtake it.

**The later keys stages, the term that was mis-sized most.** "The gain there is at least the idle (1.44) and at most down to a plain stage ... 3.0; I take 2.1 each". The stages did shrink, by 3.1 and 2.2 us; the stages behind them grew by 2.3 and 1.9. TensorE was busy 9.41 of the 10.85 [rows 3]: besides the keys' matmuls it did 36 layer products of L710 and L721, more than the 32 of a stage, and in the shorter stage of after it does 30 and the next one 35 where it did 28. So what could be won over the pair was about its idle time, and "at least the idle" was in truth near the upper end: 2.7 for both, not 4.2. The changed kernel's pairs gained 1.1, and in no run here did the two gain more than 3.0 together (2.9 in e5_half). Idle fell by 1.25 in all from x3 on, while busy time rose by 1.88, with 19 more matmuls behind x3 than before.

**GpSimd, "hidden", failed by half.** The pieces take 0.63 at a pitch of 0.70 (0.56 and 0.62 were taken), a pair of qp halves 1.77 (1.66). The chain to w was not hidden: VectorE waited 7.1 us for qp from x3 on, and TensorE 1.3 us for wk ahead of sums. The rival "GpSimd becomes the late engine" was given 0.13 and 118.7; e5_half shows 2.0 us of it from x3 on, in the first pair behind the keys stage and in the second in it, where the rival had all of it. The Trainium skill (GPSIMD Engine Reference, 4.1 Engine selection) advises VectorE for elementwise work, since GpSimd is about half as fast with two inputs; here a half of qp takes 0.85 on GpSimd and 0.56 on VectorE by their medians, a ratio of 1.5 and not 2, and the advice holds.

**The other rivals.** The PSUM input does spare the wait (e7_sbuf, e13_half_sbuf, b2_psum). The clock stayed up in the profiled execution, at 1.00 in every window from x0 on; two of the other three executions have a mean granted clock of 0.985 and 0.982 where this one has 0.997, so in them it stood lower for some time; no trace shows where. "The opening is bound by its loads" (0.12, 116.7) was near the truth but in another place: not k and v, but w_in, q and the later keys.

With e2_late's and e5_half's edits the kernel takes 115.13, and with wide dummies as well 114.95 and 114.41: about the 114.0 of the forecast, and e10_three's span of 111.9 is under its 112.5. That the sums meet is luck, for the terms don't: e10_three gains 4.5 in the opening, 5.9 from x0 to x3 and 1.9 behind it, where the forecast had 5.4, 3.1 and 3.2. What the prediction read rightly is the wait that a PSUM input spares, and the early kab; what it had wrong is the loads that now bind the opening, the stop taken as gone, GpSimd's chain as hidden, and the later keys stages at more than their idle time.
